# mLSTM cell and x·cos(x) feed-forward on one core: in the first chunk, the second gate of a slot on GpSimd, from a copy that ScalarE makes of the up product

## The chip, the core and the metric

The kernel runs on one core of a Trainium2 chip, as one launch. A core has five engines with an instruction queue each: TensorE (PE, matrix products into PSUM; PEld is its loading of the stationary operand), VectorE (DVE), ScalarE (ACT, one input, functions out of tables), GpSimd (POOL; the code uses it on SBUF data only) and SyncE (SP, which issues transfers here). Each engine works through its queue in order and waits on semaphores for the others. The metric is the device time of one execution in microseconds (us); less is better.

## The reference

The first part is an mLSTM cell over 4 batches, 8 heads, 768 steps and head size 40; the second is a feed-forward block over its 3072 output rows of 320 numbers, with 2048 hidden units:

```python
for t in range(S):
    m_new = np.maximum(f_gate[:, :, t] + m, i_gate[:, :, t])
    f_stab = np.exp(f_gate[:, :, t] + m - m_new)
    i_stab = np.exp(i_gate[:, :, t] - m_new)
    C = f_stab * C + i_stab * einsum('bhd,bhe->bhde', vt, kt)
    n = f_stab * n + i_stab * kt
    y[:, :, t] = o * einsum('bhde,bhe->bhd', C, qt) / np.maximum(np.abs(nq), 1.0)
...
h = x @ w_in          # 3072 x 320 @ 320 x 2048: the up product
g = h * np.cos(h)     # the gate
return g @ w_out      # 2048 -> 320: the down product
```

## The kernel before, in words

The 768 steps are cut into 6 chunks of 128. In each chunk the cell of a batch is computed by products (scores L546, weighed by decays at L552, then values L572 to L581 and state increments L683), 24 cells in all, numbered n. Chunk c of the feed-forward works on the 4 x 128 = 512 rows that the cells of chunk c gave, while the cells of chunk c + 1 run between its products.

The feed-forward of a chunk is 8 slots, f2 = 0 to 7, two for each cell. One slot makes two tiles (e = 0, 1) of 128 hidden units x 512 rows:

- `Up` (L713): the up product into two PSUM banks `pup` (K = 320 as 128 + 128 + 64: L731 twice, L725 for the last 64 rows). In odd slots the 64-row products of both banks come first. There are just two such banks, so the next slot's product into a bank waits until this slot has read it for the last time.
- `near` (L739, ScalarE): the up product plus 0.25 rounded to an integer, h being scaled to turns.
- `rest` (L742, VectorE): the distance to that integer. It reads the bank too.
- `sin` (L747, ScalarE): the sine of the rest, in place.
- `gate` (L751, VectorE): bank times sine, into a tile `g` of SBUF, six of them. It is the bank's last reader.

The order of all engines' queues is the order of the code: nothing rearranges it. In the first chunk (c = 0) slots 0 and 1 lie in `first_period`, slots 2 to 7 in `both_parts`. A slot's down product (`down`, L845) runs one slot later, behind the next up product.

In this chunk the weights still come in. They arrive as 64-bit numbers in halves of 32 bits and are made float32 on the way: `take_apart` (L175, L177, ScalarE), `bound` (L181, L182, VectorE), `join` (L191, VectorE) and `round_up` (L195, GpSimd). In each slot the piece of w_out is made that the down product of the next slot reads, in some slots pieces of w_in and w_in_l too. GpSimd's queue holds, besides the roundings, the fading of the states (`fade`, L666), the masking of decays (`decay_exponents`, L450), the scaling of q and k (L528, L469), copies of values (L475, L506) and the issue of transfers that bring xL for chunk 1 in place (`seam_out`, L690). VectorE also transposes q and k (L524), weighs, normalizes (L599 to L620) and adds to the states (L708).

From the third chunk on another class, `UpFast`, gives its second gate to GpSimd already (L834), out of an SBUF tile that it has for other reasons. The order of an even slot in `both_parts`, which the change's steps go through:

Of the kernel before, what the change touches and what calls it, by code (L numbers as in the profile page):

```python
# [11 lines left out]
FP = mybir.dt.float32  # L12
# [4 lines left out]
OP = mybir.AluOpType  # L17
# [12 lines left out]
def kernel(  # L30
# [20 lines left out]
    nc = tc.nc  # L51

    B, H, S, D = q.shape
    C = 128
# [130 lines left out]
    def put_together(dst, bits):  # L185
        join(dst, bits)
        round_up(dst, bits)

    def join(dst, bits):
        t = dst.bitcast(I32)  # L190
        nc.vector.scalar_tensor_tensor(out=t, in0=bits[:, 0:dst.shape[1], 1], scalar=TOP2, in1=t, op0=OP.bitwise_and, op1=OP.bitwise_or)  # L191
# [5 lines left out]
    def on_vector(made):  # L197

        for dst, bits in made:
            bound(dst)  # L200
        for dst, bits in (*made[1:], *made[0:1]):
            join(dst, bits)
        for dst, bits in made:
            round_up(dst, bits)
# [26 lines left out]
    gp = ctx.enter_context(tc.tile_pool(name="gp", bufs=6))  # L231
# [479 lines left out]
    gs, po = {}, {}  # L711

    class Up:  # L713


        def __init__(self, c, f2):
# [16 lines left out]
            if not ahead:  # L733
                low()
            self.n = [p3.tile([128, B * C], I32, name="n", tag="n") for _ in range(2)]


        def near(self, e):
            nc.scalar.activation(out=self.n[e], in_=self.pu[e], func=AF.Copy, bias=0.25)  # L739

        def rest(self, e):
            nc.vector.scalar_tensor_tensor(out=self.n[e].bitcast(FP), in0=self.pu[e], scalar=0.25, in1=self.n[e],  # L742
                                           op0=OP.add, op1=OP.subtract)
# [3 lines left out]
            nc.scalar.activation(out=r, in_=r, func=AF.Sin, scale=TWO_PI_DOWN)  # L747

        def gate(self, e):
            g = gp.tile([128, B * C], FP, name="g", tag="g")  # L750
            nc.vector.tensor_tensor(out=g, in0=self.pu[e], in1=self.n[e].bitcast(FP), op=OP.mult)  # L751
            gs[self.c, 2 * self.f2 + e] = g
# [35 lines left out]
    class UpFast(Up):  # L788
# [32 lines left out]
        def join(self):  # L821
            s, (b0, b1) = self.s, self.pu
            second = slice(HB, 2 * HB)
            nc.vector.tensor_tensor(out=b0[:, second], in0=b0[:, second], in1=s[:, 0], op=OP.add)  # L824
            self.g = gp.tile([128, B * C], FP, name="g", tag="g")
            nc.vector.tensor_tensor(out=self.g.rearrange("p (k n) -> p k n", k=2), in0=b1.rearrange("p (k n) -> p k n", k=2), in1=s[:, 0:4:3], op=OP.add)
            self.n = [p3.tile([128, B * C], I32, name="n", tag="n") for _ in range(2)]
            self.pu[1] = self.g

        def gate(self, e):  # L830
# [258 lines left out]
    def first_cells():  # L1089
# [87 lines left out]
        weigh(3)  # L1177
        values(3)
        join(*pieces[0])
        round_up(*pieces.pop(0))  # L1180
        seam_out(2)
# [368 lines left out]
```

## Time and profile before

| | us |
|---|---|
| median of 3 runs | 514.73 (512.44 to 516.18) |
| the profiled execution, device time | 514.64 |
| its span, first to last instruction | 512.9 |
| slots 2 to 7 of the first chunk | 54.9 to 123.2 of the span |
| rest of the span before / after | 54.9 / 389.7 |

How to read what follows. A line of a timeline has the start, the time that the run of equal instructions took, engine, line of the code, operation, what is written and read, the shape and the count; in brackets the engine's idle time before it and what ended that. A line of the groups has the shape, the count, and behind bars the busy sum, the mean time of one in ns, and the idle time of the engine just before them with what ended it. A row of windows has the stretch, its length, the busy time of PE, PEld, DVE, ACT and POOL with counts, the granted TensorE clock, the transfer engines' busy share and their GB/s. In the table's stretch the granted clock is 1.00.

### The profile page before, as it was taken

Reading aid. Unit: us, or ns where it says so; the run is one execution under the profiler, and the core shown is the slowest. Engines: PE = TensorE matmul, PEld = TensorE weight load, DVE = VectorE, ACT = ScalarE, POOL = GpSimd, SP = SyncE. Lnnn points to the kernel's source line nnn. Section 1 sums busy time; section 2 is a strip of 40 time slices with the busy share of each in tenths; the row PEclk is TensorE's granted clock in tenths of the full one; section 3 lists DMA queues with packets and bytes.
Section 4 is the critical chain, followed back from the end, with each engine's and each line's share of the span. In section 5 each row is a group of like instructions: output and inputs, shape, how many; then the busy total and the mean of one; then the engine's idle time right before and its main releaser. Section 6 shows DMA issues by size and latency. Waiting matters only on the chain.

```text
span 512.9 us, 11085 instructions
## 1 busy us (share of the span) xinstructions
PE 498.3 (97%) x4034; PEld 376.8 (73%) x4034; DVE 417.6 (81%) x840; ACT 325.2 (63%) x622; POOL 302.8 (59%) x390
## 2 busy tenths in 40 slices
PE   8999998999999999999999999999999999999996
PEld 6765554555675776688888688878778878787876
DVE  7887898986788887889987979998979967677655
ACT  6769779667953657747757858558858654444541
POOL 8443856544825955857576868566767455534340
PEclk9979999999999999999999999999999999999999
DMA  9978989898157527208729106828102000010001
GB/s 136 189 198 197 269 178 279 206 228 164 60 144 140 143 57 151 83 32 189 175 61 186 42 31 169 174 77 174 59 33 82 4 5 6 2 52 0 1 0 54
DMA packets 100583, 56.80 MB, mean 111 GB/s; under 512 B 63472, under 2 KB 93248, under 8 KB 100528
## 3 DMA queue, kind: packets, MB, share of 16 engines
q1 hardware_dynamic: 97408, 54.43, 45.3%
q10 hardware_dynamic: 2752, 1.23, 1.0%
q8 instruction: 32, 0.52, 0.4%
q0 software_dynamic: 368, 0.43, 0.3%
q14 instruction: 23, 0.19, 0.1%
HBM read 50.66 MB, written 4.10 MB: 107 GB/s over the span
## 4 chain that ended last, share of the span: by engine, by line
PE 73%; DVE 8%; DMA 6%; ACT 4%; SPq 3%; POOL 3%; issue 2%; DVEq 0%; ACTq 0%; POOLq 0%
PE acc L995 22%; PE pup L799 16%; PE pup L731 7%; PE pup L815 6%; PE late L995 4%; PE ps L546 4%; PE po L845 3%; PE pup L725 2%; PE vt L581 2%; PE vt L572 2%; DVE t L524 1%; PE pu L683 1%; DMA blocks<-in_moe_w_in_dram 1%; DVE n L742 1%; DMA ks<-in_k_dram 1%
## 5 line engine op out<-in xcount | busy, mean ns | idle before, releaser
L739 ACT ACTIVATE n<-pup 128x512 int32<-128x512 f32 x64 | 37.0, 594 | 95.9 <-DVE pup L824 64.7
L747 ACT ACTIVATE n<-n 128x512 f32<-128x512 f32 x96 | 58.2, 627 | 22.5 <-DVE n L742 16.2
L834 POOL TENSOR_TENSOR g<-g,n 128x512 f32<-128x512 f32 x31 | 39.6, 1276 | 52.2 <-ACT n L747 50.8
L742 DVE SCALAR_TENSOR_TENSOR n<-pup,n 128x512 f32<-128x512 f32 x64 | 43.1, 689 | 23.3 <-ACT n L739 20.8
L731 PE MATMUL pup<-xT,w_in_sb 128*128 128x512 f32 x128 | 59.2, 605 | 2.0 <-DVE g L751 2.0
L995 PE MATMUL acc<-w_out_sb,g 128*128 128x160 f32 x320 | 58.4, 302 | 0.0
L816 POOL TENSOR_TENSOR blocks<-blocks 128x256 f32<-128x256 f32 x32 | 25.7, 802 | 52.4 <-ACT blocks L808 52.4
L995 PE MATMUL acc<-T,g 128*128 128x160 f32 x304 | 55.8, 301 | 0.0
L799 PE MATMUL pup<-xT,w_in_sb 128*128 128x256 f32 x192 | 53.1, 385 | 0.4 <-ACT blocks L808 0.2
L464 ACT ACTIVATE E<-E,tab 128x128 f32<-128x128 f32 x160 | 50.2, 391 | 3.9 <-POOL E L450 3.7
L995 PEld LDWEIGHTS acc<-w_out_sb,g 128*128 128x128 f32 x320 | 49.0, 190 | 4.5 <-issue 2.7
L751 DVE TENSOR_TENSOR g<-pup,n 128x512 f32<-128x512 f32 x64 | 42.6, 687 | 7.5 <-ACT n L747 6.9
L731 PEld LDWEIGHTS pup<-xT,w_in_sb 128*128 128x128 f32 x128 | 23.3, 191 | 33.2 <-issue 31.1
L995 PEld LDWEIGHTS acc<-T,g 128*128 128x128 f32 x304 | 46.0, 190 | 0.9 <-issue 0.4
L799 PEld LDWEIGHTS pup<-xT,w_in_sb 128*128 128x128 f32 x192 | 33.8, 189 | 9.7 <-ACT blocks L808 5.9
L799 PE MATMUL pup<-x_room,room 128*128 128x256 f32 x128 | 38.2, 380 | 0.0
L824 DVE TENSOR_TENSOR pup<-pup,blocks 128x256 f32<-128x256 f32 x32 | 13.9, 436 | 29.2 <-PE pup L815 26.0
L807 ACT COPY blocks<-pup 128x512 f32<-128x512 f32 x32 | 18.6, 580 | 29.5 <-PE pup L799 27.8
L845 PE MATMUL po<-w_out_sb,g 128*128 128x320 f32 x128 | 36.3, 436 | 1.0 <-POOL w_out_sb L195 1.0
L528 POOL TENSOR_TENSOR qG<-t,G 128x512 f32<-128x512 f32 x20 | 25.9, 1295 | 18.7 <-DVE t L524 16.8
L995 PE MATMUL acc<-T,blocks 128*128 128x160 f32 x160 | 36.2, 308 | 0.0
L815 PE MATMUL pup<-xL,w_in_l 64*128 64x512 f32 x128 | 36.1, 641 | 0.0
(219 smaller groups left out, 1219.6 us busy)
## 6 DMA issues: line engine op xcount, KB each, us to landing
E<-M_d SPq DMA_DIRECT2D x20, 512.0 KB
qr<-in_q_dram SPq DMA_DIRECT2D x72, 80.0 KB
kr<-in_k_dram SPq DMA_DIRECT2D x72, 80.0 KB
bits<-in_moe_w_out_dram SPq DMA_DIRECT2D x8, 640.0 KB
G<-G_d SPq DMA_DIRECT2D x18, 256.0 KB
blocks<-in_moe_w_in_dram SPq DMA_DIRECT2D x32, 128.0 KB
out_dram<-o_sb SPq DMA_DIRECT2D x23, 160.0 KB
o<-in_o_gate_dram SPq DMA_DIRECT2D x40, 80.0 KB
```

Of the source, the lines that this page charges most:

```text
L464: nc.scalar.activation(out=Es[n][:, h], in_=Es[n][:, h], func=AF.Exp, scale=-1.0, bias=tab[:, c, 0, g:g + 1])
L528: nc.gpsimd.tensor_tensor(out=qG, in0=qkT[n][0], in1=Gs[n], op=OP.mult)
L731: nc.tensor.matmul(pu.rearrange("p (b t) -> p b t", b=B), w_in_sb[:, i, ts(2 * f2 + e, 128)], xT[c][:, i:NK * B:NK], start=(i == 0 and not ...
L739: nc.scalar.activation(out=self.n[e], in_=self.pu[e], func=AF.Copy, bias=0.25)
L742: nc.vector.scalar_tensor_tensor(out=self.n[e].bitcast(FP), in0=self.pu[e], scalar=0.25, in1=self.n[e], op0=OP.add, op1=OP.subtract)
L747: nc.scalar.activation(out=r, in_=r, func=AF.Sin, scale=TWO_PI_DOWN)
L751: nc.vector.tensor_tensor(out=g, in0=self.pu[e], in1=self.n[e].bitcast(FP), op=OP.mult)
L799: nc.tensor.matmul(bank[:, part].rearrange("p (b t) -> p b t", b=B // 2), w[:, f2], x, start=start, stop=stop, skip_group_check=True)
L815: nc.tensor.matmul(pu, w_in_l[r, f2], xL[c][r].rearrange("p b t -> p (b t)"), start=False, stop=True, skip_group_check=True)
L834: tt(out=self.g, in0=self.g, in1=self.n[e].bitcast(FP), op=OP.mult)
L845: nc.tensor.matmul(po[c][b], gs[c, f][:, ts(b, C)], w_out_sb[:, f], start=(f == 0), stop=(f == NF - 1))
L995: nc.tensor.matmul(a, lhs, rhs, start=start, stop=stop)
```

## The change

In slots 1 to 7 of the first chunk (c == 0, f2 > 0) ScalarE copies the second bank into a `g` tile, behind both `near` instructions of the slot. The second gate is then a product of two SBUF tiles on GpSimd, in place in that tile, where VectorE multiplied bank and sine before. The first gate, slot 0 and all other chunks stay as they are (`UpFast.join` sets the flag to False since it does not use this constructor).

```diff
@@ class Up, __init__
             self.n = [p3.tile([128, B * C], I32, name="n", tag="n") for _ in range(2)]
-
+            self.copied = c == 0 and f2 > 0
 
         def near(self, e):
             nc.scalar.activation(out=self.n[e], in_=self.pu[e], func=AF.Copy, bias=0.25)
+            if e == 1 and self.copied:
+                self.g = gp.tile([128, B * C], FP, name="g", tag="g")
+                nc.scalar.copy(out=self.g, in_=self.pu[e])
...
         def gate(self, e):
+            if e == 1 and self.copied:
+                nc.gpsimd.tensor_tensor(out=self.g, in0=self.g, in1=self.n[e].bitcast(FP), op=OP.mult)
+                gs[self.c, 2 * self.f2 + e] = self.g
+                return
             g = gp.tile([128, B * C], FP, name="g", tag="g")
             nc.vector.tensor_tensor(out=g, in0=self.pu[e], in1=self.n[e].bitcast(FP), op=OP.mult)
             gs[self.c, 2 * self.f2 + e] = g
@@ class UpFast, join
             self.n = [p3.tile([128, B * C], I32, name="n", tag="n") for _ in range(2)]
+            self.copied = False
             self.pu[1] = self.g
```

## The prediction

> **What bounds the kernel now.** First the page: the span is 512.9 us of a profiled run of 514.64 us, so 1.74 us lie around it; the median of the runs shown, 514.73, is 0.09 us above that run, and I carry my sum from 514.64. Then the windows, because only the first chunk (slots 0 to 7, f2 being the slot) is changed. The row below holds slots 2 to 7:
>
> ```profile
> span 512.9 us, 11085 instructions
> PE 498.3 (97%) x4034; PEld 376.8 (73%) x4034; DVE 417.6 (81%) x840; ACT 325.2 (63%) x622; POOL 302.8 (59%) x390
> ...
> 54.90:123.20 68.30, 64.96 (x433) 37.63 (x434) 58.41 (x120) 50.60 (x95) 39.54 (x50) 1.00 0.91 225
> ```
>
> TensorE (PE) is busy 64.96 of 68.30 us; the 3.34 us left are all that any relief in this stage can win. VectorE (DVE) is next with 58.41, GpSimd (POOL) has 39.54. The TensorE timeline says where the idle time lies, with its releaser in brackets:
>
> ```profile
> 54.94 3.67 PE L731 MATMUL pup<-xT,w_in_sb 128*128 128x512 f32 x8 [0.30 <-DVE g L751]
> 61.17 4.57 PE L845 MATMUL po<-w_out_sb,g 128*128 128x320 f32 x16 [0.54 <-POOL w_out_sb L195]
> 67.94 1.72 PE L725 MATMUL pup<-xL,w_in_l 64*128 64x512 f32 x4
> 73.76 4.58 PE L845 MATMUL po<-w_out_sb,g 128*128 128x320 f32 x16 [0.47 <-POOL w_out_sb L195]
> 79.72 3.67 PE L731 MATMUL pup<-xT,w_in_sb 128*128 128x512 f32 x8 [1.39 <-DVE g L751]
> 84.98 1.16 PE L546 MATMUL ps<-t,t 40*128 40x128 f32 x16 [0.52 <-DVE t L524]
> 102.10 3.67 PE L731 MATMUL pup<-xT,w_in_sb 128*128 128x512 f32 x8 [0.32 <-DVE g L751]
> ```
>
> These are up products (L725, L731), down products (L845) and scores (L546). Two waits are for GpSimd's rounding of w_out, one for transposes, three for a gate. The 1.72 at 67.94 is a hidden wait: elsewhere the same four take 1.06 to 1.13. Both banks' products run together there, on different halves of the rows, and here the second bank waited for its own gate. From 102.10 on, TensorE stands without a gap in this view, and the chain of waits lies on it up to 199.5: what is lost or won by 102.10 arrives at the end.
>
> **The change, part by part.** Sizes come from the groups of instructions: the gate on VectorE, the same shape with both inputs in SBUF on GpSimd (later chunks), and ScalarE's (ACT) PSUM copy of that shape.
>
> ```profile
> L751 DVE TENSOR_TENSOR g<-pup,n 128x512 f32<-128x512 f32 x64 | 42.6, 687 | 7.5 <-ACT n L747 6.9
> L834 POOL TENSOR_TENSOR g<-g,n 128x512 f32<-128x512 f32 x31 | 39.6, 1276 | 52.2 <-ACT n L747 50.8 <-DVE g L751 1.4
> L807 ACT COPY blocks<-pup 128x512 f32<-128x512 f32 x32 | 18.6, 580 | 29.5 <-PE pup L799 27.8 <-POOL g L834 1.3
> ```
>
> Slots 1 to 7 lose a VectorE gate (queue spacing 0.60, so 7 x 0.60 = 4.2 us), gain a ScalarE copy (7 x 0.58 = 4.1) and a GpSimd gate (7 x 1.28 = 8.9). None of these sums is on TensorE; what matters is each queue.
>
> *ScalarE.* The copy stands between the second nearest number and the first sine. In slots 1, 3, 5 ScalarE idles 1.15, 3.58 and 1.78 us there, in slots 4, 6 and 7 the gate stands behind other VectorE work (weigh, state) that ends later anyway: cost 0. In slot 2 there is no cover: gate 0 waited 0.66 us for its sine, so it comes 0.58 later, and so does the taking apart of the next weights, which VectorE awaits (it idled 0.22 us at 69.64 for it).
>
> *The up bank.* The second bank is free after the copy and not after the gate. Gates follow each other by 0.60 us, and in even slots the first bank's product (0.86 us) comes first, so nothing waits for the second gate. Only the 67.94 entry gains: 1.72 - 1.1 = 0.6 us.
>
> *GpSimd's queue.* The order of the code puts the new gate of slot 1 behind the w_in roundings and ahead of fade, mask and the rounding of w_out:
>
> ```profile
> 55.45 0.73 POOL L195 TENSOR_TENSOR w_in_l<-w_in_l,blocks 128x256 int32<-128x256 int32 x1
> 56.15 1.78 POOL L666 TENSOR_TENSOR st<-st,tab 40x128 f32<-40x128 f32 x4
> 58.01 1.58 POOL L450 TENSOR_SCALAR_AFFINE_SELECT E<-E 128x1024 f32<-128x1024 f32 x1
> 59.56 1.56 POOL L195 TENSOR_TENSOR w_out_sb<-w_out_sb,bits 128x640 int32<-128x640 int32 x1
> ```
>
> There is no hole in that queue, and its last entry releases TensorE at 61.17. A gate of 1.28 us from 56.19 pushes the rounding from 61.12 to at most 62.4; the mask, 1.58 here against 1.09 at other places, may give 0.5 back. So the down product starts 0.8 to 1.3 later; I take 1.0, nearer the full queue. In slot 2 the gate also goes ahead of two xL DMA issues (66.20), which then leave at about 69.6, 3.4 us later; xL is first read at 126, so 0. In slots 3 to 7 GpSimd idles 1.9 to 7.0 us near the gate's place.
>
> *VectorE beside GpSimd.* Some VectorE instructions stretch while GpSimd works. The timeline's same small instructions, with and without:
>
> ```profile
> 55.75 0.46 DVE L602 SCALAR_TENSOR_TENSOR d<-dt,least 128x8 f32<-128x8 f32 x1
> 60.11 1.29 DVE L612 TENSOR_TENSOR og<-og,d 128x256 f32<-128x256 f32 x1 [0.69 <-ACT og L372]
> 72.28 0.17 DVE L602 SCALAR_TENSOR_TENSOR d<-vt,least 128x8 f32<-128x8 f32 x1
> 72.93 0.42 DVE L612 TENSOR_TENSOR og<-og,vt 128x256 f32<-128x256 f32 x1
> ```
>
> The stretched ones (both inputs in SBUF) end as the GpSimd instruction beside them ends. Taking apart's scalar step L181 took 0.63 at 74.97 beside a fade, against 0.41 to 0.42. The new gate runs just where VectorE, freed of it, comes to L181 and L182. Per slot VectorE therefore gains between 0.6 (no meeting) and loses up to 0.7 (it stands 1.3 behind a gate that just began). I take 0 in slots 4 to 7, the middle, and the meeting in slots 1 and 2. The Trainium skill, SBUF — State Buffer, section Who interferes with whom, says that GpSimd and VectorE share a port pair as an exclusive lock, held for a whole instruction; by that rule each meeting costs the full rest of a GpSimd gate, and by a mere slowing of the kind of L181's 0.2 us the sum below would be 0.4 lower. The stretched L612 agrees with the lock.
>
> *The sum on TensorE.* Slot 2: the down product ends +1.0; values and increments follow; the up product of slot 3 starts at 68.9, later than gate 0 (67.88 + 0.58 = 68.46), so ScalarE's delay is hidden here; it gets 0.6 back: +0.4 at 73.7. VectorE's join of w_out moves by 0.58 (ScalarE) to 1.1 (a meeting at 68.4 to 69.6), so the down product of 73.76 starts at 74.4 to 74.9, and the same queue sets gate 0 of slot 3: the up product of 79.72 starts at 80.3 to 80.8. Here ScalarE's 0.58 is bare. Then VectorE saves 0.6 or loses 0.7 before the transposes (84.92), while TensorE's up product ends at 80.55 + 4.7 = 85.3: the 0.52 idle before the scores is eaten first, leaving +0.3 to +1.3, middle +0.8, at 85. TensorE is then closed up to 101.78. The 0.32 idle before 102.10 absorbs part only if gate 0 of slot 5 comes earlier, which by the zero above it doesn't: TensorE's 101.78 + 0.8 then passes 102.10 by 0.5, the low end by 0. Against that, slot 5's own VectorE queue can be up to 0.7 late. I forecast +0.6, between 0.2 and 1.5: 514.64 + 0.6 = **515.2 us**.
>
> **Rivals.** (a) *All hidden*: no meetings, mask gives its 0.5 back, the saved 0.6 cancels ScalarE's 0.58 in slot 3: within 0.2 of 514.6. For it: the idle rows of GpSimd in slots 3 to 7. (b) *The relief gets through*: gates 0 of slots 3 and 5 come early, and the waits of 1.39 and 0.32 and the hidden 0.6 vanish: 2.3 us less at best, 512.3; half of it, 513.5, is its likely place. For it: VectorE is the busiest engine beside TensorE and closed from 86.5 to 102. Against: in slots 2 and 3 it waits for ScalarE, which gets longer. (c) *The lock decides*: the gate of slot 3 reaches GpSimd between VectorE's two scalar steps (80.4) and holds the transposes back 1.3, as the gates of slots 4 and 5 do w_out and w_in: +1.3 in slot 1, +1.0 in slot 2, +1.3 in slot 3, less the 0.6 regained: about +3, 517.6. It decides if the scalar step's start falls after the gate's. (d) *GpSimd falls behind in every slot*: all 8.9 us on the path, 523.5; its 39.54 of 68.30 busy speaks against.
>
> **How the numbers follow.** Forecast 0.42, (a) 0.22, (b) 0.16, (c) 0.16, (d) 0.04. The runs before span 512.44 to 516.18, so a measured median can stand 1 us off by itself. The range goes from (b)'s best, 512.3, to (c) and that 1 us, 518.6; outside lie (d) and the edges of (b) and (c). Over 1% means 5.1 us, about what a measurement of this kernel can tell from no change: (d) and a little of (c) reach it upward, 0.06; downward TensorE's 3.34 us idle forbid it but for scatter, 0.03.
>
> **What would show it.** Right: the rounding of w_out that now ends at 61.12 ends at 62 or later and TensorE's wait there is over 1 us; the four products now at 67.94 take 1.1; the wait now at 79.72 grows; L181 behind a gate takes over 0.8. Wrong: TensorE's idle sum from slot 2 to slot 7 below 3.3 us (b), or above 6 (c, d); or a difference first seen after slot 7, where nothing is changed.

## The result, and the profile after

| | before | after |
|---|---|---|
| median of 20 runs each | 513.36 (512.44 to 516.18) | 516.42 (515.4 to 519.85) |
| ratio | | 1.0056 [1.0039, 1.0072] |
| profiled execution, device time / span | 514.64 / 512.9 | 515.41 / 513.6 |

The changed kernel is slower by about 2.9 us (2.0 to 3.7 by the interval), 0.56%. That is within 1%, and the time lies in the predicted range. The forecast of +0.6 had the sign right and the size too small.

The two profiled executions differ by only 0.7 us of span. The one of before is 1.3 us above its median, the one of after 1.0 below. Part of this scatter can be seen. In ScalarE's timeline of before there is a wait for the transfer of `o`, the output gate's input, which the trace of after doesn't have:

```profile
57.73 1.28 ACT L372 ACT_TABLE_LOAD   x1 [1.68 <-DMA o<-in_o_gate_dram]
```

It lies in the stage of interest, and the part on the prediction comes back to it. Below, traces therefore serve to see which wait appears where, and the medians say what it is worth.

The page's head and the windows of the changed kernel, columns as before the prediction:

```profile
span 513.6 us, 11086 instructions
PE 499.7 (97%) x4034; PEld 378.0 (74%) x4034; DVE 419.0 (82%) x833; ACT 328.1 (64%) x629; POOL 312.2 (61%) x397
...
54.90:123.20 68.30, 64.95 (x431) 38.09 (x430) 59.64 (x112) 51.99 (x100) 48.14 (x57) 0.98 0.92 222
64.00:66.00 2.00, 2.00 (x5) 1.35 (x4) 1.97 (x4) 1.83 (x3) 1.85 (x2) 0.50 0.62 117
```

VectorE has lost seven instructions (840 to 833) that took 4.2 us of its queue, and yet its busy time in the stage rose from 58.41 to 59.64. The second window shows a granted clock of 0.50 at 64 to 66 us.

TensorE's timeline of the changed kernel, at the places that the prediction quoted and at one new wait:

```profile
59.79 1.16 PE L546 MATMUL ps<-t,t 40*128 40x128 f32 x14 [0.54 <-DVE st L708]
62.38 6.26 PE L853 MATMUL po<-w_out_sb,g 128*128 128x320 f32 x16 [1.44 <-POOL w_out_sb L195]
70.72 1.13 PE L725 MATMUL pup<-xL,w_in_l 64*128 64x512 f32 x4
75.31 4.47 PE L853 MATMUL po<-w_out_sb,g 128*128 128x320 f32 x16
79.62 3.60 PE L731 MATMUL pup<-xT,w_in_sb 128*128 128x512 f32 x8
85.44 1.16 PE L546 MATMUL ps<-t,t 40*128 40x128 f32 x16 [1.17 <-DVE t L524]
102.07 3.60 PE L731 MATMUL pup<-xT,w_in_sb 128*128 128x512 f32 x8
```

Slot 2's down product waits 1.44 us instead of 0.54, a new wait of 0.54 has come ahead of it, and it then takes 6.26 us instead of 4.57. TensorE is 2.9 us late there (62.38 + 6.26 = 68.64 against 65.74). That lateness covers three waits of before: the hidden one in the four products (1.72 to 1.13), 0.47 ahead of the next down product and 1.39 ahead of slot 3's up product, both gone. (The first two, as the part on the prediction shows, belong to some executions of that code and not to all.) At 79.62 TensorE is where it was. Then slot 4's scores wait 1.17 instead of 0.52.

What VectorE meets, in its timeline, a meeting with the gates of slots 1, 3 and 5 each:

```profile
56.09 1.39 DVE L181 TENSOR_SCALAR w_out_sb<-w_out_sb 128x640 f32<-128x640 f32 x1
...
78.79 0.69 DVE L758 TENSOR_TENSOR g<-pup,n 128x512 f32<-128x512 f32 x1
79.40 1.45 DVE L181 TENSOR_SCALAR w_in_l<-w_in_l 128x256 f32<-128x256 f32 x1
...
103.07 1.40 DVE L181 TENSOR_SCALAR w_out_sb<-w_out_sb 128x640 f32<-128x640 f32 x1
```

Slot 3's scalar step as it was in VectorE's timeline of before:

```profile
80.09 0.28 DVE L181 TENSOR_SCALAR w_in_l<-w_in_l 128x256 f32<-128x256 f32 x1
```

And GpSimd's timeline:

```profile
55.88 1.25 POOL L754 TENSOR_TENSOR g<-g,n 128x512 f32<-128x512 f32 x1
57.10 2.37 POOL L666 TENSOR_TENSOR st<-st,tab 40x128 f32<-40x128 f32 x4
60.60 1.73 POOL L195 TENSOR_TENSOR w_out_sb<-w_out_sb,bits 128x640 int32<-128x640 int32 x1
67.48 1.29 POOL L754 TENSOR_TENSOR g<-g,n 128x512 f32<-128x512 f32 x1 [1.63 <-ACT n L750]
68.71 1.38 POOL L690 DMA_DIRECT2D xL<-xT  x2
...
79.40 1.29 POOL L754 TENSOR_TENSOR g<-g,n 128x512 f32<-128x512 f32 x1
```

In slot 3 GpSimd's gate and VectorE's scalar step start together at 79.40. The scalar step, 0.28 before, takes 1.45 and ends 0.16 after the gate. The Trainium skill, SBUF — State Buffer, section Who interferes with whom, calls the port pair of the two engines a lock that the first holds for its whole instruction; the trace agrees.

### The profile page after: what moved, and what is told of

Its sections match the earlier page's. It is cut to its first block, busy times and chain, and to the rows that moved or that the text cites. A ratio compares the mean times of both kernels' runs of the same rounds, so it can differ in the third digit from the quotient of the medians.

```text
span 513.6 us, 11086 instructions
## 1 busy us (share of the span) xinstructions
PE 499.7 (97%) x4034; PEld 378.0 (74%) x4034; DVE 419.0 (82%) x833; ACT 328.1 (64%) x629; POOL 312.2 (61%) x397
## 4 chain that ended last, share of the span: by engine, by line
PE 68%; ACT 7%; DMA 7%; DVE 6%; POOL 6%; issue 3%; SPq 2%; DVEq 0%; POOLq 0%; ACTq 0%
PE acc L1003 21%; PE pup L806 16%; PE pup L822 6%; PE pup L731 5%; PE late L1003 4%; PE ps L546 3%; PE po L853 3%; DMA bits<-in_moe_w_out_dram 2%; PE vt L581 2%; DVE n L745 2%; DVE t L524 2%; PE vt L572 2%; PE pup L725 1%; ACT E L464 1%; DMA qr<-in_q_dram 1%
## 5 line engine op out<-in xcount | busy, mean ns | idle before, releaser
L745 DVE SCALAR_TENSOR_TENSOR n<-pup,n 128x512 f32<-128x512 f32 x64 | 43.3, 689 | 24.1 <-ACT n L739 20.4
L758 DVE TENSOR_TENSOR g<-pup,n 128x512 f32<-128x512 f32 x57 | 38.4, 688 | 7.2 <-ACT n L750 6.6
L853 PE MATMUL po<-w_out_sb,g 128*128 128x320 f32 x128 | 37.9, 451 | 1.4 <-POOL w_out_sb L195 1.4
```

Of the source, the lines that this page charges most:

```text
L853: nc.tensor.matmul(po[c][b], gs[c, f][:, ts(b, C)], w_out_sb[:, f], start=(f == 0), stop=(f == NF - 1))
```

## The experiments

Four groups of kernels, each against runs of the kernel before on the same chip (medians 513.42, 513.30, 513.95 and 513.13 of 23, 13, 29 and 17 runs). The last column is (ratio - 1) x 513.4. All but e6 start from the changed kernel.

| kernel | what is changed in it | median, runs | ratio to before | us |
|---|---|---|---|---|
| e1 | slots 2 to 7 | 518.17, 6 | 1.0087 [1.0053, 1.0121] | +4.5 |
| e2 | slot 1 alone | 514.33, 12 | 1.0017 [0.9997, 1.0037] | +0.9 |
| e3 | copies alone, gate on VectorE | 514.31, 12 | 1.0015 [0.9993, 1.0037] | +0.8 |
| e4 | slot 2's scores twice | 517.91, 6 | 1.0089 [1.0055, 1.0122] | +4.6 |
| e5 | xL transfers of slot 2 ahead of the gates | 516.33, 6 | 1.0063 [1.0040, 1.0085] | +3.2 |
| e6 | kernel before, xL of slot 2 later | 518.75, 6 | 1.0119 [1.0095, 1.0144] | +6.1 |
| e7 | slots 3 to 7 | 516.23, 6 | 1.0062 [1.0037, 1.0086] | +3.2 |
| e8 | slots 2 to 7 and xL ahead | 515.30, 8 | 1.0043 [1.0026, 1.0059] | +2.2 |
| e11 | slots 3 to 7, k transposes ahead of the taking apart | 514.08, 12 | 1.0008 [0.9988, 1.0028] | +0.4 |
| e13 | slots 3 to 7, copy behind the sines | 515.31, 12 | 1.0033 [1.0010, 1.0057] | +1.7 |
| e9 | slots 2 to 7 with all these mended | 515.28, 12 | 1.0029 [1.0010, 1.0048] | +1.5 |
| e14 | as changed, xL ahead, k transposes ahead | 514.97, 12 | 1.0039 [1.0020, 1.0058] | +2.0 |

### Is it slot 1, and the queue of GpSimd?

The first theory took the most visible rows for the cause: the down product that waits 1.44 and then runs at half clock. Slot 1's gate makes both.

```diff
e1 -            self.copied = c == 0 and f2 > 0
e1 +            self.copied = c == 0 and f2 > 1
e2 +            self.copied = c == 0 and f2 == 1
```

> The change in slots 2 to 7 alone; slot 1 has its second gate on VectorE again. Theory A (slot 1's gate in GpSimd's queue, ahead of fade, mask and the rounding of w_out, delays the down product of slot 2 by 1.2 us, and TensorE, left idle, then runs that product at half its granted clock, +1.7 us): of the change's +2.9 us nearly all goes; between -0.5 and +0.8 us against before, no half clock between 55 and 70 us. Theory B (the meetings of GpSimd's gates with VectorE's scalar steps in slots 3 to 6 cost it): +2 to +3 us stay. Theory C (ScalarE's copies cost it): 6 of 7 copies stay, so +2 to +3 us stay.

> The change in slot 1 alone; slots 2 to 7 have their second gate on VectorE. Theory A: +2.2 to +3.2 us against before, with TensorE idle 1.2 to 1.6 us ahead of the down product at about 61 us, and a stretch of granted clock 0.5 behind it. Theories B and C: within 0.6 us of before.

Slot 1 alone costs 0.9 us, with no change inside its interval. Without it the kernel was not faster: 518.17, +4.5, with an interval (2.7 to 6.2) that overlaps the changed kernel's. So the theory falls: slots 2 to 7 carry a loss of this size by themselves, and slot 1's gate, by delaying TensorE, may hide some of it. In e1 VectorE's timeline has a wait that the changed kernel's lacks:

```profile
74.96 0.56 DVE L620 TENSOR_TENSOR xT<-vt,oT 128x384 f32<-128x384 f32 x1 [1.42 <-DMA xL<-xT]
```

This instruction writes the next cell's columns of xT; the transfer to xL reads its source from the same columns, so the write has to stand until the transfer has landed. The prediction had looked only at xL's reader at 126 us.

### Is it the copies?

In e3 the copies are made and not used; the second gate stays on VectorE, out of the bank.

```diff
-                nc.gpsimd.tensor_tensor(out=self.g, in0=self.g, in1=self.n[e].bitcast(FP), op=OP.mult)
+                nc.vector.tensor_tensor(out=self.g, in0=self.pu[e], in1=self.n[e].bitcast(FP), op=OP.mult)
```

> ScalarE's seven copies stay (their content is not used), all gates are on VectorE, out of the bank. Theory A: -0.3 to +0.6 us against before, since GpSimd's queue is that of before; the 0.58 us of slot 2 is the upper end. Theory C: +2 us or more. Theory B: as before.

+0.8 us with no change inside the interval: a small part at most. The larger part comes with the gate's move to GpSimd.

### Is it the half clock?

e4 repeats slot 2's scores into the same banks, with the same result, so that TensorE has work while it waits for the rounding.

```diff
             if cell and i == 0:
                 scores(n)
+                if (c, f2) == (0, 2):
+                    scores_again(n)
```

> The changed kernel, and the scores of slot 2 are computed a second time into the same banks (16 more products, about 0.9 to 1.1 us of TensorE), where TensorE now waits 1.44 us for the rounding of w_out. Theory A with the clock as part of it: the wait stays but TensorE is busy in it, the clock stays at 1.0, and the down product takes 4.6 us and not 6.3: 1.2 to 1.9 us faster than the changed kernel, that is +1.0 to +1.7 us against before. Theory A without the clock (only the wait counts): the same +2.9 us as the change. Theories B and C: the same, or up to 1.1 us slower.

The first reading is right at its place: TensorE's timeline of e4 has the down product at full speed, 4.57.

```profile
62.53 4.57 PE L860 MATMUL po<-w_out_sb,g 128*128 128x320 f32 x16 [0.55 <-POOL w_out_sb L195]
...
80.86 1.10 PE L738 MATMUL pup<-xT,w_in_sb 128*128 128x512 f32 x2 [2.32 <-DVE n L752]
82.27 4.46 PE L738 MATMUL pup<-xT,w_in_sb 128*128 128x512 f32 x6 [0.32 <-DVE g L765]
```

But the kernel was 4.6 us slower than before, no better than the changed one, and by its median above what any of the theories had for it. The time that TensorE got back was lost at 78 to 82: VectorE's timeline of the same execution has the wait for the transfer, and the half clock has moved to the up product behind it (4.46 for six products; 3.60 for eight at full clock). In this execution the transfer also took longer to land, 8.0 us against 5.1 in the one of after.

```profile
77.43 0.56 DVE L627 TENSOR_TENSOR xT<-vt,oT 128x384 f32<-128x384 f32 x1 [2.76 <-DMA xL<-xT]
```

### What do the late transfers cost?

e5 moves slot 2's two xL issues ahead of its gates in the changed kernel, e8 does so in e1, and e6 moves them back in the kernel before, behind part of the taking apart.

```diff
e5, e8 +                if (c, b) == (0, 1):
e5, e8 +                    seam_out(B)
                 for e in range(2):
                     up.sin(e)
                     up.gate(e)
         -                if (c, b) == (0, 1):
         -                    seam_out(B)
...
                     on_vector(made[0:2])
e6 +                    if b == 1:
e6 +                        seam_out(B)
```

> The kernel before (all gates on VectorE, no copies) with the same line moved the other way: slot 2's xL transfers are issued behind the roundings of that slot, at about 75 us and not 66. Theory D: L620 of slot 3, due at 74.5, waits until they land 3 to 8 us after their issue, so 3 to 9 us of VectorE idle there, and +3 to +8 us against before. Theories A, B and C: within 0.6 us of before, since no gate and no copy is moved.

> The changed kernel with one line moved: in slot 2 the two xL transfers are issued ahead of the gates, so GpSimd sends them at about 66 us as before the change and not behind its gate at 68.7. Theory D (slot 2's gate delays these transfers; their source is the last column block of xT, which the next cell's L620 overwrites, so VectorE waits in slot 3 until they have landed, and TensorE's next up product waits for VectorE): no idle time before L620 at about 74 us, and +0.0 to +1.2 us against before. Theory A (slot 1's queue): what it has shown alone, +0.9, so the same as D. Theory B (meetings with VectorE's scalar steps in slots 3 to 6): +2.5 us or more stay.

> Slots 2 to 7 as in the changed kernel, slot 1 as before, and slot 2's xL transfers ahead of the gates: both costs found so far taken out. Theory D: the +4.5 us that slots 2 to 7 alone had shown falls to between -0.5 and +0.8 us against before. Theory B: it stays above +2.5 us.

e6, the kernel before with nothing but this delay, is 6.1 us slower, inside the 3 to 8 that were expected. GpSimd's, VectorE's and TensorE's timelines of it:

```profile
73.00 1.20 POOL L690 DMA_DIRECT2D xL<-xT  x2
...
76.91 0.56 DVE L620 TENSOR_TENSOR xT<-vt,oT 128x384 f32<-128x384 f32 x1 [4.33 <-DMA xL<-xT]
...
81.84 5.39 PE L731 MATMUL pup<-xT,w_in_sb 128*128 128x512 f32 x8 [5.39 <-DVE g L751]
```

So the mechanism is shown, and its price is large. e1 and e8 differ in the place of these issues alone: 1.0087 and 1.0043, about 2.3 us, though their intervals just overlap, and e8 has no wait ahead of L620. e8's +2.2 is neither the -0.5 to +0.8 nor the more than +2.5 that were expected: the transfers are a part of the loss, and a loss remains without them. But in the changed kernel itself the same edit won nothing (e5, 1.0063 beside 1.0056): there the transfers land at 74.15, L620 comes at 74.40, and TensorE is late from slot 1's gate anyway. Two delays that cover each other can't be added, and taking one away shows the other.

### What do slots 3 to 7 cost alone?

```diff
+            self.copied = c == 0 and f2 > 2
```

> The change in slots 3 to 7 alone. Theory D: the transfers leave at 66 us again; what remains are the meetings of GpSimd's gates with VectorE's scalar steps (L181 took 1.45, 1.01, 1.40 and 0.68 in slots 3 to 6 against 0.3 to 0.5), which reach TensorE only through the transposes: -0.3 to +0.8 us against before. Theory B: +2.5 us or more.

+3.2 us, what theory B had expected and not D: without slot 1 and without slot 2's late transfers a loss of the whole size is there. TensorE's timeline of e7 at slot 4:

```profile
84.95 1.16 PE L546 MATMUL ps<-t,t 40*128 40x128 f32 x16 [1.74 <-DVE t L524]
```

The scores wait 1.74 us for the transposes where they waited 0.52. e1, e5 and e8, which have slot 3's gate too, have 1.76, 1.73 and 1.75. On VectorE, from the start of gate 0 of slot 3 to the end of the q transposes, before took 6.03 us (78.89 to 84.92), after 6.60 and e7 6.59: the 0.60 that the removed gate saves is lost in the meeting, and 0.57 more. Only these 0.57 are a loss: the up product ahead of the scores began at 77.64 in e7, 0.67 us ahead of gate 0, and at 79.72 in before, 0.83 behind it, so most of the longer wait is time that TensorE had won just before. Two ways of mending follow.

### The transposes beside the gate

In e7 VectorE's scalar steps meet the gate. e11 lets slot 3's k transposes, which stood behind those steps, come first.

```diff
+            self.copied = c == 0 and f2 > 2
...
-                    on_vector(made[0:-1])
                     turn_blocks(n + 1, "k")
+                    on_vector(made[0:-1])
                     on_vector(made[-1:])
```

> Slots 3 to 7 alone (which were +2.9 us), and in slot 3 VectorE transposes k ahead of the scalar steps of w_in_l, so that GpSimd's gate runs beside the transpose and not beside a scalar step. Theory L (the meeting in slot 3 is what reaches TensorE: L181 took 1.45 there, and the scores waited 1.74 us for the transposes behind it): L181 of w_in_l takes 0.3 to 0.5, the wait before the scores at about 85 us falls to 0.3 to 0.7, and the whole is 0.7 to 1.5 us faster than slots 3 to 7 without this, that is +1.4 to +2.2 us against before. Theory M (the copy's place costs it, next kernel): as slots 3 to 7, +2.9 us.

VectorE's and GpSimd's timelines of e11 and, last, TensorE's:

```profile
77.34 1.12 DVE L524 STREAM_TRANSPOSE t<-kr 128x512 f32<-128x512 f32 x1
77.34 1.30 POOL L754 TENSOR_TENSOR g<-g,n 128x512 f32<-128x512 f32 x1
78.31 0.49 DVE L181 TENSOR_SCALAR w_in_l<-w_in_l 128x256 f32<-128x256 f32 x1
...
82.86 1.16 PE L546 MATMUL ps<-t,t 40*128 40x128 f32 x16 [1.09 <-DVE t L524]
```

A transpose beside the gate takes 1.12, what it takes elsewhere (1.10 to 1.12), and the scalar step behind it, which meets only the gate's last 0.33, 0.49 instead of 1.45. The stretch from gate 0 to the q transposes is 6.06, and the loss falls from 3.2 to 0.4 us, with no change inside the interval. That is more than the 1.4 to 2.2 that were expected to be left, and more than the rows account for: the stretch is 0.53 shorter than in e7. The intervals of e7 (1.9 to 4.4) and e11 (-0.6 to 1.4) don't meet. The same order without any gate on GpSimd was not run, so how much of it the order would win by itself stays open.

### The copy's place

By the rows of the changed kernel the second nearest number has no completion signal of its own and the copy behind it gives it for both: VectorE's second L745 waits until the copy is done (0.31, 0.31 and 0.76 us in slots 4, 6 and 7 of the changed kernel; the profile names the copy in slots 4 and 7, and another engine in slot 6). e13 puts the copy behind the sines.

```diff
         def near(self, e):
             nc.scalar.activation(out=self.n[e], in_=self.pu[e], func=AF.Copy, bias=0.25)
-            if e == 1 and self.copied:
-                self.g = gp.tile([128, B * C], FP, name="g", tag="g")
-                nc.scalar.copy(out=self.g, in_=self.pu[e])
...
         def gate(self, e):
             if e == 1 and self.copied:
+                self.g = gp.tile([128, B * C], FP, name="g", tag="g")
+                nc.scalar.copy(out=self.g, in_=self.pu[e])
                 nc.gpsimd.tensor_tensor(out=self.g, in0=self.g, in1=self.n[e].bitcast(FP), op=OP.mult)
```

> Slots 3 to 7 alone, and ScalarE's copy stands behind the slot's second sine and not behind its second nearest number. In the changed kernel the second nearest number has no completion of its own: the copy signals for both, so VectorE's second rest waits 0.58 us longer (0.31, 0.31 and 0.76 us of VectorE idle show in slots 4, 6 and 7). Theory M (this costs it): those idle times vanish, 0.5 to 1.5 us faster than slots 3 to 7 without this, +1.4 to +2.4 us against before. Theory L: nothing of the meeting in slot 3 changes (GpSimd's gate comes 0.6 later and meets the next scalar step): +2.5 to +3.5 us.

Those waits are gone from slots 4 and 6 (the two `rest` of slot 4 follow each other, 1.29 us for both), and the kernel stands at +1.7, between e7 and e11 and where theory M had put it; its interval (0.5 to 2.9) overlaps e7's, so a gain is likely and not shown. The meeting in slot 3 is still there (L181 1.38, a wait of 1.52 ahead of the scores). The copy there also lets the gate start later, so this is no clean measure of the signal alone.

### All mended, and the two moved lines

e9 changes slots 2 to 7, with the edits of e5, e11 and e13, and puts the odd slots' seam_out behind their gates.

```diff
+            self.copied = c == 0 and f2 > 1
...
-                if cell:
+                if cell and c > 0:
                     seam_out(n)
...
+                if c == 0:
+                    seam_out(n)
```

> Slots 2 to 7, with everything found so far mended: slot 1 as before, the xL transfers of slot 2 ahead of the gates, k transposed ahead of the scalar steps in slot 3, GpSimd's gate ahead of the xL transfers in odd slots (so that it ends before VectorE's next scalar step), and the copy behind the sines. If theories A, D, L and M together are the whole of the cost: between -1.0 and +0.8 us against before. If something else in the gates on GpSimd costs: +1.5 us or more.

+1.5 us, not better than e11, and just what was expected if something else in the gates on GpSimd costs. TensorE's timeline shows what came in their place:

```profile
73.68 4.57 PE L852 MATMUL po<-w_out_sb,g 128*128 128x320 f32 x16 [1.33 <-POOL w_out_sb L195]
...
127.69 1.42 PE L725 MATMUL pup<-xL,w_in_l 64*128 64x512 f32 x4 [0.83 <-DMA xL<-xT]
```

The down product at 73.68 waits 1.33 for w_out's rounding, 0.47 in before. The rounding started at 72.07, when VectorE's join (71.12, 0.82 long) was done; VectorE was late, for it waited 1.00 us for ScalarE's taking apart, which now stands behind the copy, and then met slot 2's gate (L181 1.52). And slot 7's xL, issued late at 123.0, is now late for its reader.

e14 is the changed kernel with the two moves of e5 and e11 and nothing else.

> The changed kernel whole (slots 1 to 7), with two things moved: the xL transfers of slot 2 ahead of the gates, and in slot 3 the transpose of k ahead of the scalar steps of w_in_l. If the wait for these transfers (theory D) and the meeting in slot 3 (theory L) are what most of the change's +2.9 us is: +0.3 to +1.5 us against before, no idle time before L620 at 74 us, L181 of w_in_l at 0.3 to 0.5, and the wait before the scores at about 85 us under 1.2; the rest is slot 1's queue, +0.9 alone. If something else in seven gates on GpSimd carries the cost: +2 us or more.

+2.0: above the 0.3 to 1.5 that were expected if these two were most of it, and at the bound of "something else in seven gates". Its interval (1.0 to 3.0) overlaps the changed kernel's (2.0 to 3.7), so that the two moves win anything in the whole change isn't shown. The scores of slot 4 wait 0.60, nothing waits for xL, and the rows of slot 1 are back with their half clock (a wait of 1.43, then 6.26 us). No version beat the kernel before; the best, e11, is not told apart from it.

## Why the prediction came out as it did

**The bound.** Right: every loss that was found is a wait of TensorE for VectorE or GpSimd in slots 2 to 7, or a slower clock behind one. TensorE's busy time in the stage is the same (64.95 beside 64.96), though 1.7 us of it are now the half clock. The relief of rival (b) did not reach the end: in e7 the up product did start earlier, but VectorE got fuller and its transposes came later.

**GpSimd's queue in slot 1.** Right in mechanism, and about in size: the rounding ends at 62.33 ("to at most 62.4"), and the down product starts 1.21 later (0.8 to 1.3; I took 1.0). Counted from the rounding of w_in_l that stands ahead of the gate (55.45 and 55.17) it is 1.49, since the fades took longer too. Not predicted: the fades behind the gate delay the state and give the scores a 0.54 wait, and the half clock behind the two waits adds 1.7 in this execution (none in e5's, which has the same two waits, 0.56 and 1.43). On the median all this is worth +0.9 (e2), with no change inside the interval; in e2's trace the waits of 0.47 and 1.39 are gone, taken up by this lateness.

**The bank.** The four products take 1.13, as forecast, but that was luck. e6, e11 and e13, whose slots 1 and 2 have both gates on VectorE, have 1.13 too; the 1.72 stands in before, e3 and e7, whose ScalarE waited 1.60 to 1.68 us for the transfer of `o`.

**ScalarE.** "Here ScalarE's 0.58 is bare", slot 3's up product at 80.3 to 80.8: wrong in the trace, it starts at 79.62 without a wait, since TensorE came late to it. So one of the signs named for being right, a longer wait there, did not come. "In slots 4, 6 and 7 ... cost 0": not quite, for the copy gives the second nearest number's signal (0.31 to 0.76). Copies alone cost +0.8 on the median (e3), not told apart from none.

**The xL transfers.** "xL is first read at 126, so 0" was wrong as a rule: a transfer holds its source too. What it cost in the changed kernel is small (e5), 2.3 us without slot 1's gate (e1 against e8).

**VectorE beside GpSimd.** This is the step that failed in size. I took the meeting in slots 1 and 2 and "0 in slots 4 to 7", and for slot 3 the middle of -0.6 to +0.7 ahead of the scores. There were meetings in all of slots 1 to 6 (L181 at 1.39, 1.00, 1.45, 1.01, 1.40, 0.68; the "what would show it" list had over 0.8), and slot 3's had nearly the upper end: +0.57 net in the rows. That is close to rival (c): its slot, though the gate meets the first scalar step and doesn't fall between the two; its total of 517.6, +3 for the whole change, is what the medians show, though not by its sum (slot 1's +1.3 is not paid at the end).

The middle was not a fair guess, for the rows of before fix the place. GpSimd's xL issue of slot 3 ends at 79.45 there (78.33 + 1.12), and L181, at 80.09, comes at 79.49 once the second gate's 0.60 is gone. In after both start at 79.40, and in e1, e4, e5, e7 and e8, which keep this order, within 0.02 us of each other.

That this meeting is the largest part of the 2.9 us is not shown. By medians the order of one line is worth most of what slots 3 to 7 lose (3.2 to 0.4), but the rows show 0.5 of it, and with the same line moved e9 and e14 stay at +1.5 and +2.0.

**The sum.** The range held; the forecast of +0.6 was a fifth of what the medians show. The profiled execution of after lost 0.57 us from slot 2's first weigh to the end (449.38 against 448.81), which looks like the forecast and is chance: 0.39 of it lies behind the stage (from the up products at 123.57 and 123.19 to the end). e7's lost 1.34, 0.85 of it there. The medians say 2.9 and 3.2.

Part of the difference is likely in the trace of before itself. From the up product at 54.94 to the down product at 73.76 it took 18.82 us. e11, e13 and, but for the xL issues, e6 have the same code up to there and waited 0 to 0.31 for `o` instead of 1.68; they took 17.64 to 17.66, without the 1.72 at the four products and without the 0.47. e3 and e7, with a late `o`, have the 1.72 and the 0.47 too. So about 1.2 us that the prediction read as waits of the kernel belong to executions with a late `o`. A trace of the kernel before in which `o` comes early is missing, so how much of the rest this explains stays open.

It is not the half clock alone: among the executions with a mean granted clock of 1.000, 15 of the 17 of before lie between 511.25 and 512.86 (the other two at 515.53 and 515.77), the one of after at 515.85, e5's at 515.18, e7's at 515.41, e14's four between 514.16 and 514.84, and e11's at 512.10. Where the remaining 1.9 to 2.3 us arise in the typical execution stays open.

## What to carry to other kernels

When work moves to another engine, ask which instructions of the old engine will now run at the same moment, and put one there that the two don't contend for: one moved line took the loss of slots 3 to 7 from 3.2 to 0.4 us. Where the new instruction will start can often be read off the rows of before, and then no middle need be taken. Before reading waits off one execution, compare it with its median: 1.2 us of those used here are not in every execution. Of each transfer that leaves later, look at who next writes its source as well as who reads its target. Of costs that hide each other, medians of single edits don't add (0.9 for slot 1, 2.3 for the transfers and 2.8 for the moved line make 6.0, where the whole is 2.9).

## What the runs showed of the hardware

- A half clock after short gaps, by a fixed grid. In each trace the changes of the granted clock lie whole multiples of 3.41 us apart. In after TensorE was busy for 1.83 us of the window from 59.65 to 63.06, and from 63.06 to 66.47 the clock was 0.50, and 16 products took 6.26 instead of 4.57. Of the windows with such gaps between 58 and 87 us, those with 1.10 (e4), 1.37 (e6), 1.44 (e14), 1.66 (e2, e8) and 1.83 us busy were followed by one of 0.50, those with 1.98 (e5), 2.06 (e7), 2.08 (e9), 2.10 (before) and 2.27 (e1) were not. So where a gap falls decides: a gap of 1.75 us inside one window brought the half clock in e8, and gaps of 1.73 to 1.76, cut in two by the grid, brought none in e1, e5 and e7. Busy time alone is not the rule: from 28.92 to 32.34 TensorE was busy for 3.33 us in after, and 0.50 followed. The Trainium skill, TensorE: Matmul & The Clock Gate, Part 1, tells of a free-running window of about 3.4 us and half rate after an idle one; the 3.41 us and the half rate agree, but here a window busy for 1.83 us was enough.
- The small xL transfers take 2 to 8 us from issue to landing, issued by the same queue: 64.41 to 66.9 in e8, 68.71 to 73.78 in after, 69.00 to 77.0 in e4.
- VectorE's transposes don't contend with GpSimd's product (1.12 beside it in e11), its scalar step does (1.45 against 0.28).
